# Global V rows copied on chip by VectorE, and the casts and first scores of an attention front moved

## The chip, the cores and the metric

One core of one Trainium2 chip. Times are device microseconds (us) of one execution. The profile also gives the span, from the first to the last instruction of the program, which is 1.7 to 1.9 us shorter than the time. The experiments ran in four calls on four chips; kernels of one call can be compared directly, those of different calls only roughly. PE is TensorE, DVE VectorE, ACT ScalarE, POOL GpSimd, SP SyncE.

## The reference, cut to what matters

Attention over 4 batches, 8 heads, 768 positions, head size 64, in which each query sees 8 global keys and the last 96 keys, with a linear distance bias; then a gated feed-forward on 3,072 tokens.

```python
rel = pos[:, None] - pos[None, :]
is_global = pos[None, :] < n_global                  # 8
is_local = (rel >= 0) & (rel < n_local)              # 96
keep = is_global | is_local
scores = np.where(keep, scores + bias, -1e9)
a = np.exp(scores - max); a = a / a.sum()
attn = a @ v
x = attn.transpose(0, 2, 1, 3).reshape(B * S, H * D) # 3072 x 512
out = (np.maximum(x @ w_gate, 0) * (x @ w_val)) @ w_out   # d_ff 1536
```

## The kernel before

Keys and values are held in 7 blocks of 128 rows. Each block has 8 global rows and up to 120 local ones, so the same 8 global V rows stand in every block. Work goes by half batches ("halves"; half 0 and half 1 are batch 0) and by four pairs of heads. The front, half 0, is a hand-written order, because every engine starts empty. These are the parts that the change and the argument touch:

```python
qk_psum = tile_pool(name="qkps", bufs=3, space=PSUM)   # 3 + 2 + 3 = all 8 PSUM banks
av_psum = tile_pool(name="avps", bufs=2, space=PSUM)
ff_psum = tile_pool(name="ffps", bufs=3, space=PSUM)

def load_v_globals(b):                 # 8 rows from DRAM into block 0, GpSimd's queue
    nc.gpsimd.dma_start(out=v_dst(b, 0, NG, 0), in_=v[b, :, 0:NG, :].rearrange("h p d -> p h d"))

def spread_v_globals(b, j0=1, j1=NT):  # block 0 -> blocks j0..j1-1, one transfer each, SyncE's queue
    for j in range(j0, j1):
        nc.sync.dma_start(out=v_dst(b, 0, NG, j), in_=v_dst(b, 0, NG, 0))

def copy_v_globals(eng, b, j0, j1):    # the same by an engine; used later for blocks 4 to 6
    t = vbuf[b % 2][0:NG, :, D:].rearrange("p j (h z) -> p j h z", z=2 * D)[:, :, :, 0:D]
    eng.tensor_copy(t[:, j0:j1], t[:, 0:1].to_broadcast([NG, j1 - j0, H, D]))

# piece_cast: fp32 -> bf16 of one pair's k or q;  piece_t: 6 transposes on PE
# piece_copy: kT and qT out of PSUM, DVE;         piece_bias: 8 bias products into 3 banks
# piece_biased: scores onto the bias, then 3 exponents on ACT
# piece_av_wide: row sums and V products of a pair (PE);  piece_norm_wide: ln, exp (ACT), multiply (DVE)

... # loads of globals, V blocks 0..3, half 1's k and q, gate and value weights on GpSimd's queue
warm_up(8)
cast(0, 0, V, V)
piece_t(0, 0); piece_bias(0, 0); zero_more(); piece_copy(0, 0)
piece_bias(0, 1)
cast(0, 1, V, V)
piece_scores(0, 0)
... # casts of pair 2 on ScalarE between the exponents of pair 0
cast(0, 3, V, V)
spread_v_globals(0, 1, 4)
piece_bias(0, 2); piece_biased(0, 2); piece_t(0, 3); piece_bias(0, 3); piece_copy(0, 3)
piece_av_wide(0, 0, *QKB); piece_norm_wide(0, 0)     # needs the V rows of blocks 0..3
piece_biased(0, 3)
... # then pairs 1 to 3, transposes of half 1, gate products
```

The softmax here doesn't subtract the row's maximum and nothing guards it: scores larger than these inputs give would overflow.

## Time and profile before

| | before |
|---|---|
| time, median of 3 (then of 4) | 252.88 (252.74) us |
| the profiled execution: time, span | 253.76, 252.0 us |
| PE busy | 96% of the span |
| PE waits for the V transfers in the front | 4.3 us, three times |
| half clock in the front | 17.2 to 24.0 us |

### The profile page before, as it was taken

Reading aid. Unit: us, or ns where it says so; the run is one execution under the profiler, and the core shown is the slowest. Engines: PE = TensorE matmul, PEld = TensorE weight load, DVE = VectorE, ACT = ScalarE, POOL = GpSimd, SP = SyncE. Lnnn points to the kernel's source line nnn. Section 1 sums busy time; section 2 is a strip of 40 time slices with the busy share of each in tenths; the row PEclk is TensorE's granted clock in tenths of the full one; section 3 lists DMA queues with packets and bytes.
Section 4 is the critical chain, followed back from the end, with each engine's and each line's share of the span. In section 5 each row is a group of like instructions: output and inputs, shape, how many; then the busy total and the mean of one; then the engine's idle time right before and its main releaser. Section 6 shows DMA issues by size and latency. Waiting matters only on the chain.

```text
span 252.0 us, 4856 instructions
## 1 busy us (share of the span) xinstructions
PE 242.0 (96%) x1740; PEld 146.5 (58%) x1740; DVE 137.4 (55%) x359; ACT 156.5 (62%) x324; POOL 90.7 (36%) x212
## 2 busy tenths in 40 slices
PE   8839999999999999999999999999999999999995
PEld 4618566656555566655665566555665566556644
DVE  6824876796622277634763457815664466614410
ACT  7727785537665477747775587647776578643321
POOL 8982970690783035700646125700740000000000
PEclk9985999999999999999999999999999999999999
DMA  6999999999399384846562986847361200021002
GB/s 186 180 174 121 150 206 304 189 96 259 79 168 184 124 258 98 123 87 208 144 146 25 198 243 114 107 101 235 102 146 44 83 0 3 1 83 44 0 23 102
DMA packets 76223, 32.37 MB, mean 128 GB/s; under 512 B 55624, under 2 KB 72904, under 8 KB 76200
## 3 DMA queue, kind: packets, MB, share of 16 engines
q0 software_dynamic: 34368, 10.27, 36.6%
q1 hardware_dynamic: 41832, 21.81, 32.0%
q8 instruction: 13, 0.21, 0.4%
q14 instruction: 10, 0.08, 0.1%
HBM read 28.38 MB, written 6.29 MB: 138 GB/s over the span
## 4 chain that ended last, share of the span: by engine, by line
PE 72%; DVE 1%; ACT 1%; issue 0%; DVEq 0%
PE ff_ps L511 37%; PE ff_ps L534 24%; PE av_ps L432 5%; PE qk_ps L404 5%; PE ff_ps L549 1%; DVE xT L452 0%; DVE ht L527 0%; ACT rcp L446 0%; ACT lnd L441 0%; ACT grelu L520 0%; DVE es L416 0%; DVE osb L554 0%; DVEq L554 0%
## 5 line engine op out<-in xcount | busy, mean ns | idle before, releaser
L511 PE MATMUL ff_ps<-xT,wg 128*128 128x384 bf16 x384 | 77.9, 326 | 0.4 <-DVE ht L527 0.4
L511 PE MATMUL ff_ps<-xT,wv 128*128 128x384 bf16 x384 | 78.1, 326 | 0.0
L520 ACT ACTIVATE grelu<-ff_ps 128x384 bf16<-128x384 f32 x96 | 46.8, 490 | 33.9 <-PE ff_ps L511 16.2
L527 DVE TENSOR_TENSOR ht<-ff_ps,grelu 128x384 bf16<-128x384 f32 x96 | 53.2, 555 | 21.9 <-PE ff_ps L511 20.2
L534 PE MATMUL ff_ps<-wo_sb,ht 128*128 128x512 bf16 x276 | 63.2, 379 | 0.3 <-DVE ht L527 0.3
L416 DVE TENSOR_TENSOR es<-es,m_all 128x432 bf16<-128x432 bf16 (+5 forms) x118 | 34.0, 319 | 34.3 <-ACT es L407 32.9
L511 PEld LDWEIGHTS <-wv 128*128 128x128 bf16 x384 | 36.3, 98 | 22.1
L511 PEld LDWEIGHTS <-wg 128*128 128x128 bf16 x384 | 35.9, 97 | 22.6 <-issue 0.8
L407 ACT ACTIVATE es<-qk_ps 128x432 bf16<-128x432 f32 (+2 forms) x78 | 41.0, 532 | 8.5 <-PE qk_ps L404 6.2
L452 DVE TENSOR_TENSOR xT<-av_ps,rcp 64x384 bf16<-64x384 f32 x48 | 26.7, 555 | 34.0 <-ACT rcp L446 23.3
L534 PEld LDWEIGHTS <-ht 128*128 128x128 bf16 x276 | 26.0, 97 | 28.4 <-issue 0.4
L441 ACT ACTIVATE lnd<-av_ps 64x384 f32<-64x384 f32 x48 | 23.3, 485 | 13.1 <-PE av_ps L432 12.3
L360 POOL CAST kc<-ks 128x384 bf16<-128x384 f32 x20 | 9.6, 522 | 60.6 <-DMA ks<-in_k_dram 60.6
L539 ACT COPY osb<-ff_ps 128x512 f32<-128x512 f32 x23 | 13.5, 586 | 24.5 <-PE ff_ps L534 24.3
L149 POOL DMA_DIRECT2D vbuf<-in_v_dram x29 | 24.8, 862 | 5.8 <-PE av_ps L466 5.4
L404 PE MATMUL qk_ps<-qT,kT 128*128 128x432 bf16 (+5 forms) x118 | 26.5, 286 | 0.0
L432 PEld LDWEIGHTS <-vbuf 128*128 128x128 bf16 x216 | 17.8, 98 | 6.4
L432 PE MATMUL av_ps<-es,vbuf 128*128 128x216 bf16 (+4 forms) x216 | 20.5, 226 | 0.0
L404 PEld LDWEIGHTS <-kT 128*128 128x128 bf16 x118 | 11.4, 98 | 8.0
L368 POOL CAST qz<-qs 128x192 bf16<-128x192 f32 x40 | 12.7, 367 | 3.3 <-DMA qs<-in_q_dram 3.3
L446 ACT ACTIVATE rcp<-lnd 128x384 f32<-128x384 f32 x24 | 12.5, 523 | 0.8
L280 POOL COPY kT<-kN 128x240 bf16<-128x240 bf16 x12 | 5.0, 417 | 6.7 <-DMA kN<-kc 6.7
(106 smaller groups left out, 159.3 us busy)
## 6 DMA issues: line engine op xcount, KB each, us to landing
out_dram<-osb SPq DMA_DIRECT2D x23, 256.0 KB
ks<-in_k_dram SPq DMA_DIRECT2D x5, 768.0 KB
qs<-in_q_dram SPq DMA_DIRECT2D x5, 768.0 KB
vbuf<-in_v_dram POOLq DMA_DIRECT2D x23, 120.0 KB, 4.8
wg<-in_moe_w_gate_dram POOLq DMA_DIRECT2D x3, 512.0 KB, 8.4
wv<-in_moe_w_val_dram POOLq DMA_DIRECT2D x3, 512.0 KB, 10.6
wo_sb<-in_moe_w_out_dram POOLq DMA_DIRECT2D x1, 1536.0 KB, 22.8
ks<-in_k_dram SPq DMA_DIRECT2D x4, 192.0 KB
```

The costliest lines, as they stand in the source:

```text
L149: nc.gpsimd.dma_start(out=v_dst(b, NG + r0, NG + r0 + n, j), in_=v[b, :, KT * j + r0 : KT * j + r0 + n, :].rearrange("h p d -> p h d"))
L404: nc.tensor.matmul(ps[:, c : c + n_], lhsT=kt[:, j, :], rhs=qd[:, :, :, a : a + w], start=True, stop=True)
L407: nc.scalar.activation(es[:, 0:cols], ps[:, 0:cols], AF.Exp, bias=0.0, scale=scale)
L416: nc.vector.tensor_mul(e4, e4, mk)
L432: nc.tensor.matmul(av3[:, :, a : a + w], lhsT=vb[:, j, z0 : z0 + 128], rhs=es[:, c : c + NN * w].rearrange("k (n p) -> k n p", n=NN), star ...
L441: nc.scalar.activation(ln[o0 : o0 + 64], av[d0 : d0 + 64, 0:QH], AF.Ln, bias=0.0, scale=1.0)
L452: nc.vector.tensor_tensor(xT_of[s][r, p, :], av_of[s, p, e][r, 0:QH], av_of[s, p, "r"][r], op=ALU.mult)
L511: nc.tensor.matmul(st[key][:, 0:QH], lhsT=w_of(w, dc, fc), rhs=xT_of[c][:, dc, :], start=(dc == 0), stop=(dc == N_DC - 1))
L520: nc.scalar.activation(gr, psg[:, 0:QH], AF.Relu, bias=0.0, scale=1.0)
L527: nc.vector.tensor_tensor(ht[:, fc, :], psv[:, 0:QH], st["r", fc], op=ALU.mult)
L534: nc.tensor.matmul(ps2, lhsT=ht[:, fc, n * 128 : (n + 1) * 128], rhs=wo_sb[:, fc, :], start=(fc == 0), stop=(fc == N_FC - 1))
L539: nc.scalar.copy(osb, ps2)
```

## The change

Its intent: take the copies of the global V rows off the loaded transfer queues, and give VectorE, which feeds PE in the front, less to do. The casts of pair 1 go to ScalarE, those of pair 2, which are there already, go one after the other ahead of their old places, and the first scores go ahead of the second bias products so that the first exponents can start sooner.

```diff
     warm_up(8)
     cast(0, 0, V, V)
+    cast(0, 1, A, A)
     piece_t(0, 0)
     piece_bias(0, 0)
     zero_more()
     piece_copy(0, 0)
+    piece_scores(0, 0)
     piece_bias(0, 1)
-    cast(0, 1, V, V)
-    piece_scores(0, 0)
     piece_t(0, 1)
     piece_exp(0, 0, 0)
-    piece_cast(0, 2, 1, A)
+    cast(0, 2, A, A)
     piece_exp(0, 0, 1)
-    piece_cast(0, 2, 0, A)
     piece_exp(0, 0, 2)
     ...
     cast(0, 3, V, V)
-    spread_v_globals(0, 1, 4)
     piece_bias(0, 2)
     piece_biased(0, 2)
     piece_t(0, 3)
+    copy_v_globals(V, 0, 1, 4)
     piece_bias(0, 3)
```

## The prediction

> **What bounds the kernel now.** I read the page first: busy shares, the 40 slices of 6.3 us, the chain that ended last.
>
> ```profile
> PE 242.0 (96%) x1740; PEld 146.5 (58%) x1740; DVE 137.4 (55%) x359; ACT 156.5 (62%) x324; POOL 90.7 (36%) x212
> ...
> PE   8839999999999999999999999999999999999995
> ...
> PEclk9985999999999999999999999999999999999999
> ...
> PE 72%; DVE 1%; ACT 1%; issue 0%; DVEq 0%
> ```
>
> PE is the bound: from the fourth slice on it is full, and the chain from 63 us to the end is PE work. So whatever the first 19 us lose is carried whole to the end, and whatever they save comes off the end, as long as nothing later is tied to another clock (transfers are; see below). The weak spot is the third slice (PE 0.3) and the fourth, where PE is full but at half clock. Next, the table of one-us stretches (columns: stretch, length, busy time and count of PE, PEld, DVE, ACT, POOL, clock, DMA share, GB/s) and the list of waits:
>
> ```profile
> 13.00:14.00 1.00, 0.16 (x4) 0.11 (x2) 0.45 (x2) 0.95 (x2) 0.95 (x2) 1.00 1.17 146
> ...
> 16.00:17.00 1.00, 0.00 (x0) 0.00 (x0) 0.00 (x0) 0.00 (x0) 1.00 (x2) 1.00 1.44 187
> 17.00:18.00 1.00, 0.33 (x2) 0.17 (x3) 0.00 (x0) 0.00 (x0) 1.00 (x2) 0.61 1.57 188
> ...
> 23.00:24.00 1.00, 1.00 (x13) 0.88 (x10) 0.71 (x3) 0.84 (x2) 0.38 (x1) 0.50 0.55 33
> 24.00:25.00 1.00, 1.00 (x12) 0.74 (x11) 0.46 (x1) 0.37 (x1) 1.00 (x2) 0.98 0.12 14
> ```
> ```profile
> PE qk_ps L466 <- DMA vbuf<-vbuf: 4.3, 3, 3.1
> ```
>
> PE, DVE and ACT all stand still from 13.1 to 18.2 us; then PE runs at 0.50 until 24. The timeline (start, duration, engine, line) says what they stand for:
>
> ```profile
> 6.94 0.79 DVE L261 CAST qk<-qs 128x384 bf16<-128x384 f32 x1
> ...
> 7.85 0.50 ACT L261 CAST qk<-ks 128x384 bf16<-128x384 f32 x1
> ...
> 8.89 2.35 SPq L141 DMA_DIRECT2D vbuf<-vbuf  x3
> ...
> 12.75 0.71 DVE L312 COPY qT<-av_ps 64x384 bf16<-64x384 bf16 x2
> 12.79 0.11 PEld L466 LDWEIGHTS <-vbuf 128*64 128x64 bf16 x2
> ...
> 13.92 0.28 PE L466 MATMUL qk_ps<-es,vbuf 128*64 128x216 bf16 x2 [0.84 <-DMA vbuf<-vbuf]
> ...
> 17.27 0.33 PE L466 MATMUL qk_ps<-es,vbuf 128*64 128x144 bf16 x2 [3.07 <-DMA vbuf<-vbuf]
> ...
> 18.02 0.23 PE L466 MATMUL qk_ps<-es,vbuf 128*64 128x24 bf16 x2 [0.42 <-DMA vbuf<-vbuf]
> 18.19 1.18 PE L339 MATMUL ff_ps<-qT,kT 128*128 128x432 bf16 x4
> ...
> 27.32 0.68 DVE L145 COPY vbuf<-vbuf 8x1536 bf16<-8x1536 bf16 x1
> ```
>
> The first attention output (pair 0) needs the eight global V rows in key blocks 1 to 3. Three SyncE transfers of 8 KB bring them; issued from 8.89 us, they arrive one after the other at 13.9, 17.2 and 18.0. The scores of pair 3, which stand behind on PE, had their last operand at 13.46 (the qT copy, 12.75 + 0.71).
>
> **What the Trainium skill says.** "DMA: Bandwidth & Descriptors", section Issuing engines are not separate DMA queues: transfers of all issuers share the same 16 engines and interleave. The trace agrees: the 8 KB transfers took 5 to 7.4 us beside a full queue of loads (DMA share 1.2 to 2.3 from 8 to 18 us). "TensorE: Matmul & The Clock Gate", Part 1: PE drops to half clock after an idle window of about 3.4 us, and needs a busy one to come back. The trace agrees: granted clock 0.5 from about 17.2 to 24.0, two such windows. "ScalarE: Activation LUTs", What ACT_TABLE_LOAD costs: an activation takes 186 ns + 0.833 ns per element, 506 ns for 384; the ScalarE casts here took 502 and 511. "SBUF — State Buffer", Who interferes with whom: a VectorE copy in a two-port mode and GpSimd lock each other out. The 0.79 us cast beside GpSimd's issues, against 0.36 elsewhere, looks like it; the trace does not prove it.
>
> **The change, part by part.** I walk the in-order engines through the built program's new order, with the durations of the trace.
>
> (1) Casts of pair 1 to ScalarE, first scores ahead of bias 1. Before: VectorE finished qT of pair 0 at 6.63 and cast pair 1 until 7.73; PE did bias 1 from 6.08 and the scores from 7.04. After: ScalarE ends its masks at 6.25 and casts pair 1 to about 7.1. PE waits from 6.1 for qT until 6.7, does the scores to 7.3, bias 1 (1,200 columns, 0.5 us at full clock) to 7.85, the transposes to 8.45; VectorE's copies of pair 1 start at 8.48 instead of 8.17. So reordering costs about 0.3 us here: VectorE loses work but then waits for PE.
>
> (2) Casts of pair 2 next to each other on ScalarE end near 8.5 instead of 9.19. VectorE now arrives at these transposes at 9.87 (before 9.62), so this hides; the score-exponent chain of pairs 1 and 2 stays about 0.25 us late: exponents of pair 2 start at 11.68 against 11.43.
>
> (3) The copy. It moves 8 x 1,536 bf16, the same shape as the L145 copy that took 0.68 us. Its source, the rows loaded into block 0, landed near 8.9 (issue 4.08 + 4.8), so it waits for nothing and runs about 11.9 to 12.55, ahead of the copies of pair 3, which then end at 13.94 instead of 13.46. The V rows proper of blocks 1 to 3 landed by 11.3 (issues 4.82 to 7.5, 3.8 to 4.8 us each), so they do not take the place of the wait.
>
> (4) PE after that. Output of pair 0: 12.8 to 13.3, no stop. Scores of pair 3 at 14.0 instead of 18.19: **4.2 us** gained. Then at full clock: output of pair 1 (0.54 us instead of 1.08), transposes of half 1 (0.36 instead of 0.62; their loads land near 14.1), output of pair 2 at 15.4. Output of pair 3 needs a PSUM pair that pair 1 frees through ln, exp and multiply on ScalarE and VectorE; these stand behind pair 3's exponents, so its V products wait until about 17.4: one us of PE idle that the half clock had covered. Bias and scores of half 1 end at 18.7. The first gate product, at 24.82 before, then starts at about 18.7: shift **6.1 us**, that is 4.2 from the wait and 1.9 from the clock (a full 6.8 us at half clock would be worth 3.4, of which the PSUM wait eats over a third).
>
> (5) What transfers allow. They do not move with PE. The first gate weights land at 18.1 (9.66 + 8.4), needed at 18.7; keys and queries of half 1, second part, near 19.95, needed near 21.2; first value weights 22.5, needed 23.5; V blocks 4 to 6 near 24.8 and the rest of block 3 (an estimate, 25.3), needed 25.8. All hold, by 0.5 to 1.3 us. GpSimd's later loads were issued after the last output of pair 3 (23.6 us) and left the DMA nearly idle from 23 to 25; they now follow without that hole, some 3 us earlier. The queries of the next batch landed at 44.5 and would land near 41.2 to 41.6; with GpSimd's cast (0.5) the transposes can start at 41.7 to 42.1, and PE arrives at 47.9 - 6.1 = 41.8. Up to 0.3 us may be lost there. Afterwards nothing differs.
>
> Sum: 6.1 less about 0.2 = 5.9 us; 252.9 - 5.9 = **247.0 us**.
>
> **Rivals.** (a) *Only the wait counts, half clock stays or comes back elsewhere.* The new gap of PE at 6.1 to 6.7 lies in the very window (3.5 to 7.0, worked back from 17.2 in steps of 3.41) whose busyness brought full clock at 7.0. The window from 17.2 to 20.6, busy for some 70%, did not suffice; the new one is busy for some 83%. If it fails, PE stays cold until 10.4 and the front loses about 1.1 us: 248.1. I give this one in five. (b) *The V loads or gate weights become the wait.* Landing times above speak against it; margins of half a us could turn into 0.5 to 1 us of loss: 247.5 to 248. (c) *The copy holds VectorE, or GpSimd locks it out*: it lies on the path to pair 3's scores, 0.5 us already counted; twice as long costs 0.6 more: 247.6. (d) *More than summed*: without 8 KB transfers of small packets the load queue runs faster (157 to 187 GB/s while they moved, 200 just after), and the margins of (5) grow: 246.5. (e) *The gain is hidden anyway*, PE's later work waiting for something fixed in time: PE's slices are full from 19 us on with little waiting, so a time of 250 or more is unlikely.
>
> **Range and chances.** The centre is 247.0. Downward I see some 1 us (PSUM wait shorter than walked, queue faster), upward 1.5 (clock, margins): 245.8 to 248.5. Faster by over 2% means under 247.8, which is only 0.8 us above my centre: 0.76. Slower would need a new stop of 11 us: 0.01.
>
> **What would show it.** Right: no PE wait for a copied V row; the scores of pair 3 at 14.0 +- 0.3; the granted clock at 1.00 between 17 and 24; the copy at about 0.68 us ending before 12.8; the first gate product at 18.7 +- 0.7; the first transposes of the next batch at 41.9 +- 0.5. Wrong: a clock at 0.5 after 7 us, a PE wait over 0.5 us on gate weights or V blocks near 18 to 26 us, or a stop at the next batch's transposes over 0.5 us, each of which takes its length off the gain.

## The result, and the profile after

The changed kernel took 248.47 us (median of 4, 248.10 to 248.89) beside 252.74 for the kernel before. The ratio is 0.9834, with a 95% interval of 0.9809 to 0.9858. Ratios here are the mean time of one kernel's fast runs over that of the other's of the same rounds, so not quite the ratio of the medians. The gain is 4.2 us where 5.9 had been forecast: a clear gain, but under 2%, although the prediction gave 0.76 to more than that. The 248.47 us lie at the very upper edge of its range. The profiled execution took 248.15 us, with a span of 246.3.

The page's slices of the changed kernel (40 slices of 6.2 us) answer to those of before:

```profile
PE   7779999999999999999999999999999999999994
...
PEclk9999999999999999999999999999999999999999
```

The hole in the third slice is filled, and the half clock in the fourth is gone. One-us stretches of the changed kernel, with the columns as in the prediction:

```profile
13.00:14.00 1.00, 0.28 (x9) 0.25 (x4) 0.83 (x4) 0.97 (x2) 0.94 (x2) 1.00 0.84 117
16.00:17.00 1.00, 0.48 (x14) 0.35 (x10) 0.77 (x4) 0.96 (x3) 1.00 (x2) 1.00 1.45 200
17.00:18.00 1.00, 0.83 (x17) 0.77 (x18) 0.94 (x4) 0.97 (x3) 1.00 (x2) 1.00 1.58 190
```

From 13 to 18 us all engines now work, at full clock. What is left of PE's idle time here is 0.7 us before the scores of pair 3 and 0.7 us before the V products of pair 3. The timeline of the same kernel (start, duration, engine, line; idle time and releaser in brackets):

```profile
11.53 0.88 DVE L145 COPY vbuf<-vbuf 8x1536 bf16<-8x1536 bf16 x1
...
12.77 0.43 PE L466 MATMUL qk_ps<-es,vbuf 128*64 128x216 bf16 x8
...
13.92 0.67 PE L339 MATMUL ff_ps<-qT,kT 128*128 128x432 bf16 x4 [0.72 <-DVE qT L312]
...
17.17 0.45 PE L466 MATMUL av_ps<-es,vbuf 128*64 128x216 bf16 x8 [0.70 <-DVE xT L488]
...
18.77 0.65 PE L511 MATMUL ff_ps<-xT,wg 128*128 128x384 bf16 x3
```

The eight V products of pair 0 run in one go. The scores of pair 3 start at 13.92 (18.19 before) and the first gate product at 18.77 (24.82 before). Of the shift of 6.05 us there, 4.27 come from the wait. The other 1.78 come from the clock: the stretch from these scores to the gate takes 4.85 us instead of 6.63. That is close to the prediction's 4.2 and 1.9, and the two profiled spans differ by 5.7 us. Yet the timed runs differ by 4.2. So the question for the experiments was not only where the changed kernel lost its gain, but also what the kernel before does when it is not being looked at.

### The profile page after: what moved, and what is told of

It reads as the page before. It is cut to its first block, busy times and chain, and to the rows that moved or that the text cites. A ratio compares the mean times of both kernels' runs of the same rounds, so it can differ in the third digit from the quotient of the medians.

```text
span 246.3 us, 4841 instructions
## 1 busy us (share of the span) xinstructions
PE 237.2 (96%) x1732; PEld 143.5 (58%) x1740; DVE 137.0 (56%) x358; ACT 156.8 (64%) x326; POOL 90.8 (37%) x212
## 4 chain that ended last, share of the span: by engine, by line
PE 73%; DVE 1%; ACT 1%; issue 1%; DVEq 0%
PE ff_ps L511 38%; PE ff_ps L534 24%; PE av_ps L432 5%; PE qk_ps L404 5%; PE ff_ps L549 1%; DVE xT L452 0%; DVE ht L527 0%; ACT rcp L446 0%; DVE es L416 0%; ACT lnd L441 0%; ACT grelu L520 0%; DVE osb L554 0%; DVEq L554 0%
## 5 line engine op out<-in xcount | busy, mean ns | idle before, releaser
L527 DVE TENSOR_TENSOR ht<-ff_ps,grelu 128x384 bf16<-128x384 f32 x96 | 53.2, 555 | 22.2 <-PE ff_ps L511 20.6
L452 DVE TENSOR_TENSOR xT<-av_ps,rcp 64x384 bf16<-64x384 f32 x48 | 26.6, 555 | 34.2 <-ACT rcp L446 21.3
L432 PEld LDWEIGHTS <-vbuf 128*128 128x128 bf16 x216 | 17.8, 98 | 6.4
```

Of the source, the lines that this page charges most:

```text
L432: nc.tensor.matmul(av3[:, :, a : a + w], lhsT=vb[:, j, z0 : z0 + 128], rhs=es[:, c : c + NN * w].rearrange("k (n p) -> k n p", n=NN), star ...
L452: nc.vector.tensor_tensor(xT_of[s][r, p, :], av_of[s, p, e][r, 0:QH], av_of[s, p, "r"][r], op=ALU.mult)
L527: nc.vector.tensor_tensor(ht[:, fc, :], psv[:, 0:QH], st["r", fc], op=ALU.mult)
```

## The experiments

My theory: the profiled execution of the kernel before was a slow one of its kind, because the end of its wait and the stretch at half clock differ from execution to execution. The rival: the trace of before was typical, and the changed kernel loses about a us elsewhere.

### e1: the kernel before again

No edit.

> The kernel before, unchanged, for its spread. Theory 1 (the half clock of the kernel before depends on where a free-running window falls, and the profiled execution, 253.76 us, caught more of it than the timed ones, median 252.7): executions differ by 1 us or more, the longer ones with the lower mean granted clock (0.986 for 6.8 us at half clock, nearer 0.993 for one window of 3.4 us, 1.0 for none); spans from about 250.3 to 252.0. Rival (the clock part was right, and the kernel after loses a microsecond elsewhere): every execution of this kernel shows a clock near 0.986 and a span near 251 to 252.

Measured: ratio 1.0011 (0.9973 to 1.0049). In this call the kernel before, in 17 executions under its two names, took 250.22 to 253.84 us. I sorted every execution of this kernel from the timed calls (50 of them, e1 to e12) by the mean clock that the records give:

| mean clock | executions | mean time | range |
|---|---|---|---|
| 0.985 to 0.986 (half clock for 6.8 us) | 26 | 253.08 | 251.9 to 253.9 |
| 0.991 to 0.993 (about 3.4 us) | 21 | 251.71 | 250.2 to 252.8 |
| 1.0 (none) | 3 | 250.41 | 250.2 to 250.6 |

The lengths in brackets are worked out from the mean clock: 6.8 us at 0.5 in a span of 252 us make 0.9865. The theory holds as to the spread: one and the same kernel has a spread of 3.7 us, and the profiled execution at 253.76 lay at its slow end. The rival, as it was put here, falls, since 24 of the 50 executions show a higher clock. Two things stay open at this point. The profiled execution's clock, 0.986, is that of 26 of the 50, so half clock alone does not make it exceptional. And whether the changed kernel loses something elsewhere is not settled by this table.

### e2: the changed kernel again

No edit.

> The changed kernel, unchanged. Theory 1: clock 1.00 in all executions, spans 246.2 to 247.0 (the spread of the first 7 us, where the clock comes up at a time that differs from run to run), ratio to before 0.983 +- 0.002; the first gate product near 18.8 to 19.5 us. Rival: an execution at or above 247.0 shows a stop of PE after 19 us that the first profile does not have.

Measured: 248.24 us (247.97 to 248.44), ratio 0.9819 (0.9780 to 0.9859), clock 0.998 to 1.0. Its first gate product is at 18.97 and its span 246.1. The changed kernel has less of a spread; with e11 and the first result, 16 executions run from 247.68 to 249.12, mean 248.45.

### e3: the wait kept, the clock kept up

PE is given 52 small matmuls of zeros, into unused columns of a bank, to do while it waits for the V rows. They do not touch the result.

```diff
             for i, (j, a, w, m) in enumerate(todo):
+                if (s, p, what) == (0, 0, 1):
+                    for _ in range((0, 10, 38, 4)[i]):
+                        nc.tensor.matmul(av[1][:, QH:512], lhsT=warm, rhs=warm, start=False,
+                                         stop=False, skip_group_check=True)
                 for e in range(2):
```

> The kernel before with the wait for the V rows kept and PE kept busy in it by 52 small matmuls of zeros into unused columns, so that the clock stays up. Theory 1: clock 1.00; the scores of pair 3 still start near 18.2 us; against the profiled execution of before 2 us are gained, against the timed ones only what they really lost to the clock, 0.5 to 1.2 us (ratio 0.995 to 0.998). Rival: the clock part is worth 1.9 us in every execution: ratio 0.9925.

Measured: 250.59 us (250.31 to 252.30), ratio 0.9923 (0.9881 to 0.9964), clock 0.999 to 1.0. By means, 252.82 for before, 250.89 here and 248.23 in e2: **the clock is worth 1.9 us and the wait 2.7 us**. The split is rough: the interval of the ratio allows 0.9 to 3.0 us for the clock, and the six times of e3 and the six of e2 give 1.9 to 3.5 us for the wait (95%, worked out from these times). I had put 0.5 to 1.2 us on the clock here, and the mean speaks for the prediction's 1.9 instead. What was too large is the wait. The timeline of this kernel shows one reason:

```profile
16.88 0.20 PE L470 MATMUL qk_ps<-es,vbuf 128*64 128x24 bf16 x2 [0.40 <-DMA vbuf<-vbuf]
17.02 0.68 PE L339 MATMUL ff_ps<-qT,kT 128*128 128x432 bf16 x4
...
21.88 0.65 PE L515 MATMUL ff_ps<-xT,wg 128*128 128x384 bf16 x3
```

The last V rows had landed by 16.88, not 18.02, so the scores of pair 3 start 1.2 us earlier than in the first trace. From there to the gate it takes 4.86 us, the same as in the changed kernel (4.85). One limit of this experiment: the zeros themselves last until 16.49 us in this profile, so an execution whose rows land sooner would not show it here.

### e4: the copy alone

```diff
-    spread_v_globals(0, 1, 4)
     piece_bias(0, 2)
     piece_biased(0, 2)
     piece_t(0, 3)
+    copy_v_globals(V, 0, 1, 4)
     piece_bias(0, 3)
```

> The VectorE copy in place of the three transfers, casts and order as before. Both theories: the wait is gone, clock 1.00, scores of pair 3 at about 14.0; the front of the kernel is 0 to 0.3 us earlier than in the full change (reordering was reckoned to cost 0.3 us), ratio 0.981 to 0.985. If the moved casts and scores are worth something by themselves, it is above 0.986.

Measured: 248.02 us (247.75 to 248.43), ratio 0.9811 (0.9774 to 0.9847), scores of pair 3 at 13.89. The copy alone does all that the full change does (248.24).

### e5: the moved casts and scores alone

The changed kernel with `spread_v_globals(0, 1, 4)` back in its place, and without the copy.

> Casts and scores moved, the three transfers kept. Prediction's step: worth nothing or a cost of up to 0.3 us, because the wait for the V rows ends when the transfers land: ratio 0.998 to 1.002, clock again 0.986 to 0.993, scores of pair 3 at 17 to 18.2 us. Rival (the moved work is worth something by itself): ratio under 0.997.

Measured: 252.77 us (251.92 to 253.59) beside 252.41; ratio 1.0017 (0.9977 to 1.0057); clock 0.985 to 0.993; scores of pair 3 at 17.44. These parts are worth nothing that this measurement can see (the interval allows from 0.6 us gained to 1.4 us lost).

### e6: other PSUM banks, first try

In the changed kernel PE is idle for 0.7 us before pair 3's V products, because their bank is freed by pair 1's multiply. This edit gives pair 3 the banks that pair 0 used, and the bias of half 1 one bank from each of the three pools.

```diff
-        banks = [pool.tile([128, 512], FP32, name=name) for _ in range(3)]
+        pools = [(pool, name)] * 3
+        if (s, p) == (1, 0):
+            pools = [(ff_psum, "ff_ps"), (av_psum, "av_ps"), (qk_psum, "qk_ps")]
+        banks = [po.tile([128, 512], FP32, name=na) for po, na in pools]
...
     piece_copy_k(1, 0)
-    piece_mul_wide(0, 1)
     piece_copy_q(1, 0)
+    piece_mul_wide(0, 1)
     AV(0, 2, *FFB)
-    AV(0, 3)
+    AV(0, 3, *QKB)
```

> The changed kernel with the output of pair 3 and the bias of half 1 given other PSUM banks, and the qT copy of half 1 ahead of the multiply of pair 1. If the PE idle of about 0.8 us before pair 3's V products is on the path, it goes, the first gate product starts at 17.8 to 18.3 us instead of 18.8, and 0.3 to 0.6 us of the end is gained (ratio to before 0.001 to 0.003 under that of the changed kernel, 0.982 in the last call). If transfers take over (first gate weights at 17.8, the rest of block 3 at 25.1), the gain is under 0.2.

Measured: 248.16 us (247.77 to 248.91), ratio 0.9838 (0.9802 to 0.9874): no gain that shows, though the changed kernel did not run in this call (248.24 in the one before). Its first gate product starts at 18.77, where 17.8 to 18.3 was expected, since the wait only moved:

```profile
18.00 0.35 PE L327 MATMUL qk_ps<-dd,sid 128*128 128x216 bf16 x2 [0.67 <-ACT lnd L483]
```

The third bias bank came from the same pool as pair 3's output and waited for its ln. No wait for a transfer shows there; the edit missed its aim.

### e7: the global rows loaded directly

The kernel before, with blocks 1 to 3 filled from DRAM at the head of GpSimd's queue, and no second hop.

```diff
-    load_v_globals(0)
+    for j in range(4):
+        nc.gpsimd.dma_start(out=v_dst(0, 0, NG, j),
+                            in_=v[0, :, 0:NG, :].rearrange("h p d -> p h d"))
...
-    spread_v_globals(0, 1, 4)
```

> The kernel before with the global rows of blocks 1 to 3 loaded from DRAM by GpSimd at the head of its queue, in place of the second hop on SyncE. If it is the second hop behind a full queue that costs, the wait goes (V products of pair 0 by 13.5 us, clock 1.00), ratio 0.980 to 0.986. If small-row transfers are dear wherever they stand, or the 2 us of additional issues delay keys, queries and gate weights of half 1, the wait or a new one takes 1 to 3 us back: ratio 0.986 to 0.996.

Measured: 249.10 us (248.59 to 249.84), ratio 0.9876 (0.9836 to 0.9917), clock 0.998 to 1.0. The wait for V rows is gone (V products of pair 0 at 13.04), so small rows are not dear wherever they stand. In the kernel before they were issued from 8.9 us on, by SyncE, after a first landing; here from 4.04 us on, by GpSimd, straight from DRAM. Which of these differences counts, e7 does not separate. But two new waits, for what stands behind the additional issues, show up in this kernel's timeline:

```profile
16.11 0.36 PE L296 MATMUL qk_ps<-ident,qs 128*64 128x128 bf16 x6 [0.68 <-DMA qs<-in_q_dram]
...
19.69 0.66 PE L511 MATMUL ff_ps<-xT,wg 128*128 128x384 bf16 x3 [0.21 <-DMA wg<-in_moe_w_gate_dram]
```

Together 0.9 us, about what its mean is above that of e6, which has the copy (249.16 and 248.24). This is rival (b) of the prediction; in the changed kernel it did not come.

### e8: a third look at the kernel before

No edit, one profile.

> A further look at the kernel before, for the end of its wait: 18.19 and 18.11 us in the two profiled so far, 17.02 with PE kept busy. If the end of the wait differs between executions, it lies anywhere from 16.5 to 18.3 here, and the half clock begins at another time after the start of the kernel (17.2 and 16.4 so far).

Measured: 252.77 us, span 251.0, clock 0.986. One-us stretches of this execution, then its timeline:

```profile
15.00:16.00 1.00, 0.29 (x2) 0.16 (x2) 0.00 (x0) 0.00 (x0) 0.96 (x3) 0.85 1.26 184
16.00:17.00 1.00, 0.04 (x3) 0.03 (x1) 0.00 (x0) 0.00 (x0) 1.00 (x2) 0.50 1.48 186
```
```profile
17.00 0.23 PE L466 MATMUL qk_ps<-es,vbuf 128*64 128x24 bf16 x2 [0.96 <-DMA vbuf<-vbuf]
17.16 1.18 PE L339 MATMUL ff_ps<-qT,kT 128*128 128x432 bf16 x4
...
23.56 0.65 PE L511 MATMUL ff_ps<-xT,wg 128*128 128x384 bf16 x3
```

The wait ends at 17.0 and the clock falls at 15.7. The stretch before that fall, and then three stretches of the first trace, before its fall and up to its rise (length, then PE busy):

```profile
12.29:15.70 3.41, 1.50 (x23) 1.17 (x22) 1.36 (x5) 1.62 (x4) 3.22 (x10) 1.00 1.28 169
```
```profile
13.80:17.20 3.40, 0.28 (x2) 0.14 (x2) 0.00 (x0) 0.26 (x1) 3.31 (x9) 1.00 1.30 176
17.20:20.63 3.43, 2.94 (x30) 2.08 (x32) 0.56 (x1) 1.84 (x5) 1.00 (x2) 0.50 1.37 198
20.63:24.04 3.41, 3.41 (x52) 3.27 (x49) 2.46 (x8) 2.49 (x5) 0.42 (x1) 0.50 1.56 114
```

In the five profiles with the transfers the scores of pair 3 start at 18.19 (first), 18.11 (e1), 17.16 (e8), 17.44 (e5) and 17.02 (e3), mean 17.6. The half clock begins at 17.2, 16.4, 15.7 and 16.1 us, and never in e3.

### e9: other PSUM banks, second try

As e6, but the bias of half 1 takes its second and third bank from the pool that pair 1 frees, and the next transposes take theirs from the other pool.

```diff
-    AV(0, 3)
+    AV(0, 3, *QKB)
+    qk_of[1, 0] = [ff_psum.tile([128, 512], FP32, name="ff_ps")] + [
+        av_psum.tile([128, 512], FP32, name="av_ps") for _ in range(2)]
...
-    TC(1, 1)
+    TC(1, 1, *QKB)
```

> As the first run with other PSUM banks, whose third bias bank turned out to wait for the ln of pair 3; now that bank comes from the pair that pair 1 frees, and the next transposes from the other pool. If the PE idle in front of the first gate product is what delays the end, the bias of half 1 no longer waits past 17.7, the gate starts at 18.2 to 18.4 (18.8 before), and 0.3 to 0.5 us come off the end against the changed kernel of this call. If ScalarE, busy without a break from 14.3 to 20 us, sets the pace, the gate moves and later products wait: under 0.2 us.

Measured: 247.63 us (247.12 to 247.98), beside 248.87 for the changed kernel on the same chip (e11); means 247.61 and 248.65, so 0.4% less. The qT copy of half 1 goes ahead of pair 1's multiply here too, as in e6, so this gain is that of the banks and this order together. In its timeline pair 3's V products follow without a stop, and the gate starts at 18.65 although this execution's scores of pair 3 were 0.2 us later than in the first trace of the change:

```profile
14.14 0.67 PE L340 MATMUL ff_ps<-qT,kT 128*128 128x432 bf16 x4 [0.45 <-DVE qT L312]
...
16.50 0.43 PE L467 MATMUL qk_ps<-es,vbuf 128*64 128x216 bf16 x8
...
18.65 0.66 PE L512 MATMUL ff_ps<-xT,wg 128*128 128x384 bf16 x3
```

From scores to gate it is 4.5 us, against 4.85. The gate is later than I expected (18.2 to 18.4) and the gain at the end larger (1.0 against 0.3 to 0.5); part of the latter is the slower starts of e11 (see there).

### e10: scores of pair 3 ahead of the output of pair 0

```diff
-    copy_v_globals(V, 0, 1, 4)
     piece_bias(0, 3)
     piece_copy(0, 3)
+    copy_v_globals(V, 0, 1, 4)
+    piece_biased(0, 3)
     piece_av_wide(0, 0, *QKB)
     piece_norm_wide(0, 0)
-    piece_biased(0, 3)
```

> The changed kernel with the copy behind the qT copy of pair 3 and the scores of pair 3 ahead of the output of pair 0: the 0.5 us that the copy stands in front of pair 3's scores go. Scores of pair 3 at 13.0 instead of 13.9 us. If that is on the path: 0.3 to 0.5 us off the end. If ScalarE's queue behind them (three exponents, then ln and exp of each pair) sets the pace: 0 to 0.2 us.

Measured: 250.44 us (249.65 to 251.43), slower than the change by 1.8 us of means (250.48 against 248.65), the opposite of what either theory said. Its scores of pair 3 started at 13.91, not at 13.0: the qT copy they wait for ended at 13.85, so the copy of the V rows had not been what held them. Three of the six executions took 249.65 to 249.83 us with a mean clock of 0.999 to 1.0, the other three 251.05 to 251.43 with 0.991 to 0.993: it looks as if half clock came back in half of them (no such execution was profiled). Against the change's 248.65, the first three alone still lose about 1.1 us. The timeline of ScalarE in this kernel:

```profile
15.27 1.30 ACT L352 ACTIVATE es<-ff_ps 128x432 bf16<-128x432 f32 x3 [2.50 <-PE qk_ps L466]
```

The exponents of pair 3 waited for pair 0's output products, not for their own scores. The pool of exponents has three buffers, and pair 3 takes the one that pair 0's output is still reading (read from the code and this wait; no run with a fourth buffer was made). The order that looked improvable had been forced by a buffer.

### e11: the changed kernel, third time

No edit.

> The changed kernel beside the two variants on the same chip, for their comparison: ratio to before 0.980 to 0.984, spans 246.0 to 247.0, clock 1.00.

Measured: 248.87 us (247.68 to 249.12), ratio 0.9866 (0.9825 to 0.9908), clock 0.999 to 1.0. In its profile the scores of pair 3 start at 14.82 instead of 13.92; the first q cast of the front waited for its load until 4.27 (3.91 in the first profile), and several VectorE copies took longer. So the front of the changed kernel differs by up to 0.9 us too:

```profile
14.82 0.67 PE L339 MATMUL ff_ps<-qT,kT 128*128 128x432 bf16 x4 [0.90 <-DVE qT L312]
```

It is the smaller spread of the two.

### e12: the copy with the freed banks

The edit of e9 on the kernel of e4.

> The copy alone (casts and scores as before) with the freed banks of e9. The casts and the order were worth nothing in e5 and in e4 against e2. If that stays so with the freed banks, this is as fast as e9: median 247.3 to 247.9 us, clock 1.00, first gate product at 18.2 to 18.7. If the moved casts matter once the banks are free, it is 248.0 or more.

Measured: 247.39 us (246.92 to 247.55), ratio 0.9822 (0.9772 to 0.9873) to a kernel before that had many of its quicker executions (median 251.08). In time this is the fastest kernel of the study: mean 247.30, against 248.06 for e4 and 248.45 for all executions of the change, though from different calls. It has neither the moved casts nor the moved scores, and nothing shows that it misses them.

## Why the prediction was right or wrong

**What bounds it: right.** The front's losses went to the end nearly whole; the page shows PE full after 19 us in both kernels. Some readings on the way were loose: of the engines said to "stand still from 13.1 to 18.2 us", ACT was busy until 14.06 and DVE until 13.46, and the DMA share from 8 to 18 us was 1.14 to 2.34. The 506 ns for a cast is an estimate from the page's formula. And the 0.36 us casts, set against the one of 0.79 "beside GpSimd's issues", also ran beside such issues, at 6.67 and 11.03 us, so the comparison says little about a lock.

**Part (1) and (2), casts and order, a cost of some 0.3 us that hides: neither shown nor contradicted.** Alone they are worth nothing that e5 can see (ratio 1.0017, 0.9977 to 1.0057). In the first profile the copies of pair 1 started at 8.17, as before, not 8.48, since in that execution full clock came near 4.5 us instead of 7.0. The granted clock in the tables does not tell this, it reads 1.00 throughout the first 8 us; it is read from the durations of the same eight products, first in the kernel before, then in the changed one:

```profile
5.02 1.22 PE L324 MATMUL qk_ps<-dd,sid 128*128 128x216 bf16 x8
```
```profile
4.77 0.70 PE L324 MATMUL qk_ps<-dd,sid 128*128 128x216 bf16 x8
```

**Part (3), the copy: mechanism right, size off.** It waited for nothing, but took 0.88 us instead of 0.68 while GpSimd was issuing transfers. The scores of pair 3 still started at 13.92 for 14.0 foreseen: the copy could start 0.4 us earlier than walked (11.53), so two errors cancelled, which is luck.

**Part (4), the failing step.** "Scores of pair 3 at 14.0 instead of 18.19: 4.2 us gained." The mechanism was right: the copy alone takes the stop away (e4). For the pair of traces the size is right too (4.27). For executions at large this term of the sum is mis-sized: in e3 against e2, with the clock up in both, the wait is worth 2.7 us (1.9 to 3.5). Three things make up the difference. The transfers often land earlier than in the trace that I read (mean start of the scores 17.6 over five profiles). The changed kernel's own scores start at 13.92, 14.11 and 14.82, mean 14.3, so 3.3 us remain. Lastly, from the first gate product to the end the three profiles of the change took 227.5, 227.1 and 227.5 us, and e3 226.8; this last 0.3 to 0.7 us I have not traced to one cause. So the rival of the experiments was right in part: of the 1.5 us between 4.2 and 2.7, about 0.6 lie in the earlier landings of the kernel before, 0.4 in the later starts of the changed one, and the rest is not traced. The clock part of the step, 1.9 us, was measured as 1.9 (0.9 to 3.0). That the digits agree is partly luck: five of the eleven executions of the kernel before in that call show a mean clock of 0.993, one window at half clock, where the prediction read two.

**The sum.** I took a shift out of one profiled execution, at 253.76 us, and subtracted it from the median of others, at 252.88. From the execution's own time, 253.76 - 5.9 = 247.9, where its counterpart measured 248.15. About 0.9 us of the mistake was visible before anything ran: the profiled execution stood outside the range of the timed ones (252.29 to 252.96). I had read the Trainium skill's remark, on the page "TensorE: Matmul & The Clock Gate" (Part 1), that the clock's window is "free-running" and does not reset when the kernel starts, and used it only for the warm-up risk. It fits the stall as well. In the three profiles of the kernel before the clock falls at 17.2, 16.4 and 15.7 us; three windows of 3.41 us earlier are 7.0, 6.2 and 5.5 us, and that is where the products of the same fronts turn from 1.22 us for eight to 0.69 to 0.71. So the windows lie differently from one execution to the next, and the table in e1 has executions with two, one and no window at half clock. That the place of the window decides among the three is inferred: only executions with two were profiled.

**Part (5), transfers: right.** No wait for gate weights or V blocks came; the transposes of the next batch started at 41.84 in the first profile (41.8 to 42.1 foreseen).

**Rivals.** (a), a cold front after the new gap, did not happen in the three profiles of the change, whose scores of pair 0 run at full speed (0.67 us) from 6.58, 6.69 and 7.08 us. Its reason, that a window busy for "some 70%" did not suffice, rested on a misreading: the table gives 86%. (b) came only in e7. (c) was small, 0.2 us on the copy; (d) was not measured by itself. (e) did not happen. The rival that was missing is that the kernel before is better than its trace.

## What to carry to other kernels

Before a shift read from a trace is subtracted from a timed median, compare the profiled execution's own time with the timed ones; if it lies outside their range, the waits in it may not be typical, and in this kernel the waits for transfers and the clock after a stall varied most. A small transfer that depends on another transfer, on engines with a full queue, can hold PE for microseconds; here an 8-partition copy by VectorE did the same work in 0.88. When a wait goes, look for the buffer or bank that is behind it: freeing two PSUM banks (e9, with one copy moved) gave more than moving four casts and a set of scores (e5), and an order can be pinned by a buffer that no view names (e10).

## What the Trainium skill lacked or had wrong

- "TensorE: Matmul & The Clock Gate", Part 1, says in its table that the clock falls after an idle window of about 3.4 us. Here it fell after windows that were not wholly idle. In e8, PE was busy for 1.50 of the 3.41 us before the fall at 15.7 us, or 44%; in the first trace for 0.28 of 3.40. A later section of the page, on psum-queue depth-cycling, has frequent short idles bring the clock down and up, but the page gives no busy share for either direction. For the rise, the stretch of the first trace from 17.2 to 20.6 us, with PE busy for 2.94 of 3.43 us, did not suffice, and the next one, fully busy, did. The lines are shown under e8.
- The same page treats run-to-run variation as a matter of the start. With a stall in the kernel it is worth more: 253.08, 251.71 and 250.41 us as mean times for two, one and no window at half clock; part of these differences can be the wait for the rows, which also differs between executions.
- "DMA: Bandwidth & Descriptors", Anatomy of one DMA, gives about 2 us fixed cost for a transfer that GpSimd issues. Here the 8 KB load that GpSimd issued at 4.08 us, beside other loads, took 4.8 us. Three transfers of 8 KB issued from SyncE, which that figure does not cover, from 8.9 us on beside a full GpSimd queue were waited for until 13.9, 17.2 and 18.0 us, and in another execution (e8) until 13.7, 15.7 and 17.0; the page has no figure for a small transfer beside a loaded queue, nor for its spread.
- "SBUF — State Buffer", Who interferes with whom, has no size for short copies: the same 8 x 1,536 copy took 0.88 us at 11.5 us, beside two of GpSimd's issues, and 0.68 us at 21.3 us of the same execution, while GpSimd waited. That fits the lock that the page describes, but casts of 0.36 us also ran beside GpSimd's issues (see above); no run here isolates it.
